# Seven block products for z, operand sums made earlier, and a turned fold loop in an attention and two-MLP kernel on one core

## The chip, the cores and the metric

One core of a Trainium2 chip runs the whole program. The metric is device time in microseconds (us) of one execution, the median over runs. The engines are called PE (TensorE matmul; PEld is its weight load), DVE (VectorE), ACT (ScalarE), POOL (GpSimd) and SP (SyncE, which here issues every DMA).

## The reference

All data are float32. Retention attention with a causal decay per head, then a max-of-three MLP, then a gated MLP without activation:

```python
scores = scale * np.matmul(q, k.transpose(0, 1, 3, 2))       # batch 8, heads 8, seq 576, head_dim 64
x = np.matmul(scores * Dmat[None], v)                        # Dmat: gamma_h ** (i - j) for i >= j, else 0
# tokens: 8 * 576 = 4608, d_model 512
h = np.maximum(np.maximum(x @ w1, x @ w2), x @ w3)           # d_ff 768
z = h @ w_out
a, b = z @ v1, z @ v2                                        # second MLP, d_ff 1024
out = ((a * b) @ v3) @ v_out
```

The weights arrive as float64 bits and are turned into float32 in the kernel.

## The kernel before

Every float32 operand x of a matmul is split into hi (rounded by ACT, `copy_r` line 92) and lo = x - hi (`low` line 95, on DVE or POOL); a product is three matmuls, hi*hi, lo*hi and hi*lo. Five stages follow one another on PE.

1. **Attention and h**, in blocks of 512 tokens (9 blocks, `n_blk`). Sequences are cut in 40 chunks of up to 128 tokens. For each chunk SP loads q and k (four DMAs each, lines 265 to 273), v and k again; POOL scales q and v (lines 306 to 310), DVE turns q and k (line 314), PE makes scores, output and state (lines 321 to 346), ACT and DVE write the block's x as hi and lo. `products` (line 408) makes one of 18 groups per block (6 feature tiles f, 3 weights i) of 12 matmuls of 512 columns; `maximum` folds the three into `hb`, and `keep` (line 428) stores it to `h_d` in DRAM. Beside this, `convert` (line 144) brings the other weights from float64 to float32 in 46 units (`rest`, lines 229 to 236): load `raw`, two ACT and three DVE instructions, store: 6 units of w_out to `wo1_d`, 16 of the gated weights to `wp_d`, 8 of v_out to `wo2_d`, 16 of v3 to `w3t_d` (four loads each, a DVE transpose).
2. **z = h w_out**, in 12 blocks `j` of 384 tokens (lines 616 to 642): for each of 6 feature tiles k and 4 output tiles m one `product` of three matmuls of 384 columns. `load_h` and `split_h` (lines 477 to 500) keep a ring of h tiles; DVE and POOL take turns on `hl`. Beside it the sums of the gated weights are made (`sums_of`, lines 546 to 571) and then the operands of the fold are loaded.
3. **The fold** w4 = v3 v_out (lines 715 to 728): 8 output tiles m, each 8 products of 512 columns in one bank, one after another.
4. **a and b**, in 6 pairs of 384-token blocks, by seven block products in place of eight (lines 851 to 913), and a*b to `g_d`.
5. **out = g w4**, by seven block products of 256 columns (lines 951 to 977), 18 steps `s` of 84 matmuls.

Each engine runs its instructions in program order, SP's queue included. The order of the first two blocks is written out by hand in `ORDER` (lines 30 to 48); from the third block on `when(t, fn)` gives each step a due time, in units of one group of 12 matmuls (18 to a block), and steps are emitted in the order of due times (a "+" in `ORDER` takes the next of them). For a chunk whose scores are due at t the q and k loads stand at t - 6, POOL's scaling at t - 3, DVE's turns just behind.

## Time and profile before

| | us |
|---|---|
| median of 3 runs | 1321.61 |
| runs | 1320.63, 1321.61, 1325.02 |
| the profiled execution | 1317.18 |
| its span, first to last instruction | 1315.4 |
| PE busy in the span | 1296.0 |
| stage 1, up to about | 580 |
| stage 2 (z) | 580 to 731 |
| stage 3 (fold) | 731 to 775 |
| stages 4 and 5 | 775 to 1315 |

The stage times are from the chain of waits, by the tile that PE writes (`ps_h`, `ps_z`, `ps_w`, `ps_x`/`ps_y`/`ps_v`). The granted clock is 1.00 over the whole span. A busy PE includes modelled ends of matmuls, so the distance from one matmul to the next is better read as a stretch divided by its count. SP's issues are not in the table of busy time; they stand in the timeline of its queue.

### The profile page before, as it was taken

The page shows a single profiled execution, that of the slowest core. Times are in us where ns is not written, and L with a number is a line of the kernel's source. Part 1 is how long each engine was busy: PE and PEld are TensorE (multiplying, and loading weights), DVE is VectorE, ACT ScalarE, POOL GpSimd, SP SyncE. Part 2 cuts the span into 40 slices and gives each one's busy share as a digit, 9 for nine tenths or more (in the row PEclk, how much of TensorE's full clock was granted, in tenths as well). Part 3 has the DMA queues.
Part 4 walks back from the last instruction along what each step waited for, and adds up shares of the span by engine and source line. Part 5 has one row for each costly group of instructions (what it writes and reads, how often), then busy time and mean ns, then how long its engine had stood idle before and what let it go on. Part 6 is the DMA issues. An engine that isn't in the chain of part 4 may idle for free.

```text
span 1315.4 us, 24550 instructions
## 1 busy us (share of the span) xinstructions
PE 1296.0 (99%) x9464; PEld 1184.1 (90%) x9464; DVE 753.4 (57%) x1134; ACT 447.6 (34%) x878; POOL 402.2 (31%) x356
## 2 busy tenths in 40 slices
PE   7999999999999999999999999999999999999998
PEld 5878888888888888889999899999999999899998
DVE  5996556766757675227644334334333436788885
ACT  3551111322222122124434333233333324455553
POOL 2112101121111210026634334333433434644433
PEclk9999999999999999999999999999999999999999
DMA  9966567878788785237557432222232232644552
GB/s 223 232 161 131 135 148 186 222 181 210 184 183 190 167 183 134 92 104 230 180 186 235 145 123 85 73 79 73 88 99 79 73 95 72 178 155 152 168 158 93
DMA packets 347748, 193.53 MB, mean 147 GB/s; under 512 B 243056, under 2 KB 321392, under 8 KB 347632
## 3 DMA queue, kind: packets, MB, share of 16 engines
q1 hardware_dynamic: 347632, 191.97, 53.8%
q8 instruction: 74, 1.21, 0.4%
q14 instruction: 42, 0.34, 0.1%
HBM read 125.85 MB, written 66.06 MB: 146 GB/s over the span
## 4 chain that ended last, share of the span: by engine, by line
PE 93%; DMA 2%; DVE 2%; issue 1%; SPq 1%; POOL 0%; ACT 0%; DVEq 0%; POOLq 0%; ACTq 0%
PE ps_h L416 33%; PE ps_x L584 23%; PE ps_y L584 11%; PE ps_z L584 9%; PE ps_v L584 5%; PE ps_w L584 3%; PE sc L321 2%; PE o L334 2%; PE st L346 1%; PE o L340 1%; SPq L99 1%; DMA z_d<-zo 0%; DMA w<-w_d 0%; DMA raw<-in_moe_w_dram 0%; DMA a<-wp_d 0%
## 5 line engine op out<-in xcount | busy, mean ns | idle before, releaser
L416 PE MATMUL ps_h<-xh,w1h 128*128 128x512 f32 (+1 forms) x664 | 258.5, 391 | 0.0
L416 PE MATMUL ps_h<-xh,w1l 128*128 128x512 f32 (+1 forms) x664 | 254.6, 385 | 1.7 <-DVE w1l L96 1.7
L416 PE MATMUL ps_h<-xl,w1h 128*128 128x512 f32 (+1 forms) x664 | 174.1, 384 | 0.0
L416 PEld LDWEIGHTS ps_h<-xh,w1h 128*128 128x128 f32 x664 | 124.7, 188 | 29.3 <-issue 3.6
L416 PEld LDWEIGHTS ps_h<-xh,w1l 128*128 128x128 f32 x664 | 124.8, 188 | 26.1 <-DVE w1l L96 2.4
L310 POOL TENSOR_TENSOR v<-v,tables 128x512 f32<-128x512 f32 x40 | 44.7, 1117 | 329.6 <-DMA v<-in_v_dram 310.2
L416 PEld LDWEIGHTS ps_h<-xl,w1h 128*128 128x128 f32 x664 | 123.0, 188 | 24.8
L426 DVE TENSOR_TENSOR hb<-ps_h,hb 128x512 f32<-128x512 f32 (+1 forms) x110 | 74.3, 676 | 114.0 <-PE ps_h L416 113.6
L880 POOL TENSOR_TENSOR c<-c 128x384 f32<-128x384 f32 x72 | 81.9, 1138 | 174.5 <-DVE c L748 81.7
L743 ACT ACTIVATE snap<-ps_x 128x384 f32<-128x384 f32 x120 | 58.4, 491 | 190.8 <-PE ps_x L584 185.9
L584 PE MATMUL ps_z<-hh,w1oh 128*128 128x384 f32 x288 | 96.3, 334 | 0.8 <-issue 0.8
L584 PE MATMUL ps_z<-hl,w1oh 128*128 128x384 f32 x288 | 96.3, 334 | 0.3 <-DVE hl L96 0.3
L584 PE MATMUL ps_z<-hh,w1ol 128*128 128x384 f32 x288 | 96.2, 334 | 0.0
L158 ACT ACTIVATE e<-raw 128x512 f32<-128x512 f32 x64 | 42.9, 670 | 146.6 <-DMA raw<-in_moe_w_dram 96.1
L93 ACT ACTIVATE hb<-ps_h 128x512 f32<-128x512 f32 (+1 forms) x56 | 32.4, 581 | 170.1 <-PE ps_h L416 170.1
L96 POOL TENSOR_TENSOR hl<-hr,hh 128x384 fp32r<-128x384 f32 x36 | 39.3, 1093 | 78.4 <-ACT hh L93 70.6
L748 DVE TENSOR_TENSOR c<-ps_v,snap 128x384 f32<-128x384 f32 x48 | 26.6, 556 | 62.0 <-PE ps_v L584 39.9
L307 POOL TENSOR_TENSOR q<-q,tables 128x512 f32<-128x512 f32 (+1 forms) x31 | 32.7, 1054 | 91.3 <-DMA q<-in_q_dram 71.2
L328 DVE TENSOR_TENSOR p<-sc,tables 128x512 f32<-128x512 f32 (+1 forms) x80 | 47.1, 625 | 20.5 <-PE sc L321 20.3
L93 ACT ACTIVATE hh<-hr 128x384 fp32r<-128x384 f32 x72 | 36.1, 521 | 56.2 <-PE ps_z L584 24.5
L584 PEld LDWEIGHTS ps_z<-hh,w1oh 128*128 128x128 f32 x288 | 54.1, 188 | 1.2 <-issue 1.2
L584 PEld LDWEIGHTS ps_z<-hl,w1oh 128*128 128x128 f32 x288 | 54.1, 188 | 0.7 <-DVE hl L96 0.6
(215 smaller groups left out, 3353.6 us busy)
## 6 DMA issues: line engine op xcount, KB each, us to landing
g_d<-c SPq DMA_DIRECT2D x96, 192.0 KB, 1.9
raw<-in_moe_w_dram SPq DMA_DIRECT2D x34, 512.0 KB, 6.0
h_d<-hb SPq DMA_DIRECT2D x54, 256.0 KB, 3.0
gr<-g_d SPq DMA_DIRECT2D x12, 1024.0 KB, 6.0
z_d<-zo SPq DMA_DIRECT2D x12, 768.0 KB, 3.6
zr<-z_d SPq DMA_DIRECT2D x48, 192.0 KB, 3.2
out_dram<-ob SPq DMA_DIRECT2D x36, 256.0 KB, 2.1
...
```

The costliest lines, as they stand in the source:

```text
L93: nc.scalar.activation(dst, src, AF.Copy)
L96: eng.tensor_tensor(dst, full, hi.bitcast(F32), ALU.subtract)
L158: nc.scalar.activation(z["e"], raw[:, :, 1].bitcast(F32), AF.Copy, scale=2.0 ** -112)
L307: nc.gpsimd.tensor_tensor(z["q"][:, :r], z["q"][:, :r], qs[:, j, :r].unsqueeze(3).to_broadcast([P, r, G, 32]), ALU.mult)
L310: nc.gpsimd.tensor_tensor(z["v"], z["v"], vd.unsqueeze(2).to_broadcast([P, H, D]), ALU.mult)
L328: nc.vector.tensor_tensor(z[g][:c, :, :c], z["sc"][g][:c, :, :c], mask[:c, :c].unsqueeze(1).to_broadcast([c, G, c]), ALU.mult)
L416: nc.tensor.matmul(ps[:, cols], l, r, start=n == 0, stop=n == len(mms) - 1)
L426: nc.vector.tensor_tensor(hb, ps[:, cols], hb, ALU.max)
L584: nc.tensor.matmul(ps, l, r, start=start and j == 0, stop=stop and j == len(mms) - 1, skip_group_check=again)
L743: nc.scalar.activation(t, ps[:, :N2], AF.Copy)
L748: nc.vector.tensor_tensor(r, ps[:, :N2], t, ALU.add)
L880: nc.gpsimd.tensor_tensor(x, x, y, ALU.mult)
```

## The change

z is made in 9 blocks of 512 tokens, each as a 2 by 2 block product with 7 products in place of 8 (`Z_ORDER`): output features in two halves of 256, tokens in two halves of 256, the 768 features of h in two halves of 384. One product is 2 output tiles by 3 feature tiles by three matmuls of 256 columns: 18 matmuls, in two PSUM banks out of three pairs (X, V, Y). It needs h in seven forms of [128, 3, 256] per block (4 quadrants, of which one is replaced, and differences) and w_out in seven forms. Partial results are copied out by ACT (`snap_z`) and added by DVE (`keep_z`), and stored in eight pieces of 128 KB per block.

The differences of h are made on POOL beside the attention: for blocks 2 to 8 four subtractions of 256 columns per pair of feature tiles (`differences`), one of which is in place in `hb` ahead of its `keep`, and a store of 384 KB; for blocks 0 and 1 later, by two loads, four subtractions and three stores per pair (`late_differences`, six times, due in blocks 6 and 7). The feature tiles are taken in the order 0, 3, 1, 4, 2, 5 (`F_ORDER`), and the two keeps of a pair are issued together. The sums of the gated weights move from DVE in the z stage to POOL beside the conversion (`gated_unit`), and 28 finished tiles go to `ws_d` instead of 16 to `wp_d`; in the z stage they are only loaded and split (`ws_split`, 28 steps in blocks 1 to 6). The v3 units stand ahead of the v_out units, with a store of whole 2 KB runs. `raw` has 4 buffers instead of 6 and its load stands one unit earlier. All of `hl` is on DVE. The fold runs with k outside and all 8 banks open. `ORDER` is another list of the same steps. z is read back by half as many, longer loads.

```diff
 ORDER = """
-tables fv0 fq0 fk0 fv1 fq1 sv0 fk1 fv2 tq0 fq2 ga0 eq0 fk2 tk0 up0 fq3 sv1 ek0 fk3 sc0 ft0 ft1 tq1 da0 tk1 fq4 db0
...
+tables fq0 fk0 fq1 fv0 fk1 tq0 fq2 eq0 tk0 fv1 ek0 fk2 sc0 fq3 tq1 da0 sv0 db0 fq4 ou0 eq1 fv2 ft0 ga0 xh0 tk1 up0
...
-    wp_d = dram.tile([P, 2, 2, KD, 512], F32, name="wp_d")
-    h_d = [dram.tile([P, KF1, N1], F32, name=f"h_d{t}") for t in range(NT // N1)]
-    z_d = [dram.tile([P, KD, N2], F32, name=f"z_d{t}") for t in range(NT // N2)]
+    NAMES = ("a11", "a12", "a22", "s1", "s2", "s3", "s4")
+    ws_d = dram.tile([P, 2, 2, len(NAMES), 2, 256], F32, name="ws_d")
+    h_d = [dram.tile([P, KF1 // 2, 7, N1 // 2], F32, name=f"h_d{t}") for t in range(NT // N1)]
+    z_d = [dram.tile([P, KD, 2 * N2], F32, name=f"z_d{t}") for t in range(NT // N2 // 2)]
...
+    F_ORDER = [f for c in range(KF1 // 2) for f in (c, c + KF1 // 2)]
...
-            z["raw"] = cv.tile([P, 1024], I32, tag="raw", name="raw", bufs=6)
+            z["raw"] = cv.tile([P, 1024], I32, tag="raw", name="raw", bufs=4)
-            w = cv.tile([P, 512], I32, tag="w", name="w")
+            w = cv.tile([P, 512], I32, tag="w", name="w", bufs=7)
-            when(t - 3, fetch)
+            when(t - 4, fetch)
...
+    def gated_unit(t, i, c, n):
+        quads = quadrants.setdefault((i, c), {})
+        e, kk = n % 2, n // 2
+        src = words_of(f"moe2_w{i + 1}")[(2 * kk + c) * P:(2 * kk + c + 1) * P, 1024 * e:1024 * e + 1024]
+        def keep(x, w):
+            load(ws_d[:, i, :, NAMES.index(x), c], w.rearrange("p (q f) -> p q f", q=2))
+        def add(dst, x, y, op, to):
+            nc.gpsimd.tensor_tensor(quads[to], quads[x], quads[y], op)
+            quads[dst] = quads[to]
+            keep(dst, quads[dst])
+        def done(t, w):
+            x = f"a{e + 1}{kk + 1}"
+            quads[x] = w
+            if x != "a21":
+                keep(x, w)
+        convert(t, lambda raw: [(raw, src)], done)
+        if n == 3:
+            for m, sums in enumerate((("s1", "a21", "a22", ALU.add, "a22"), ("s3", "a11", "a21", ALU.subtract, "a21"),
+                                      ("s2", "s1", "a11", ALU.subtract, "a11"), ("s4", "a12", "s2", ALU.subtract, "a12"))):
+                when(t + 5.5 + 0.8 * m, add, *sums)
...
-            load(w3t_d[:, 4 * half:4 * half + 4, j, :], wt.rearrange("p (m i) -> p m i", i=P))
+        when(t + 3.2, lambda: load(w3t_d[:, j, 4 * half:4 * half + 4], z["t"].rearrange("p (m i) -> p m i", i=P)))
-    rest += [lambda t, half=half, i=i, c=c: rows_unit(
-        t, words_of(f"moe2_w{i + 1}")[c * P:(c + 1) * P, 1024 * half:1024 * half + 1024], wp_d[:, half, i, c])
-        for i in range(2) for c in (0, 2, 1, 3) for half in range(2)]
+    rest += [lambda t, i=i, c=c, n=n: gated_unit(t, i, c, n) for i in range(2) for c in range(2) for n in range(4)]
+    rest += [lambda t, j=j, half=half: w3_unit(t, j, half) for j in range(KF2) for half in range(2)]
     rest += [lambda t, k=k: rows_unit(t, words_of("moe2_w_out")[k * P:(k + 1) * P], wo2_d[:, k]) for k in range(KF2)]
-    rest += [lambda t, j=j, half=half: w3_unit(t, j, half) for j in range(KF2) for half in range(2)]
...
     def keep(t, f):
-        load(h_d[t][:, f], hbs.pop((t, f)))
+        e, c = divmod(f, KF1 // 2)
+        load(h_d[t][:, c, 2 * e:2 * e + 2], hbs.pop((t, f)).rearrange("p (n t) -> p n t", n=2))
+    def subtract(lo, hi, t2, t3, t4):
+        for to, x, y in ((t3, hi[:, 1], lo[:, 1]), (lo[:, 1], lo[:, 1], lo[:, 0]), (t2, hi[:, 1], lo[:, 1]), (t4, hi[:, 0], t2)):
+            nc.gpsimd.tensor_tensor(to, x, y, ALU.subtract)
+    diffs = {}
+    def differences(t, c):
+        d = hb_p.tile([P, 3, N1 // 2], F32, tag="d", name="d", bufs=1)
+        subtract(*(hbs[t, f].rearrange("p (n t) -> p n t", n=2) for f in (c, c + KF1 // 2)), *(d[:, n] for n in range(3)))
+        diffs[t, c] = d
+    def keep_differences(t, c):
+        load(h_d[t][:, c, 4:], diffs.pop((t, c)))
+    def late_differences(t, c):
+        x = []
+        def fetch():
+            for e in range(3):
+                x.append(cv.tile([P, 2, N1 // 2], F32, tag="w", name="w", bufs=7))
+                if e < 2:
+                    load(x[e], h_d[t][:, c, 2 * e:2 * e + 2])
+        def work():
+            lo, hi, d = x
+            subtract(lo, hi, d[:, 0], d[:, 1], hi[:, 0])
+        def store():
+            lo, hi, d = x
+            load(h_d[t][:, c, 1], lo[:, 1])
+            load(h_d[t][:, c, 4:6], d)
+            load(h_d[t][:, c, 6], hi[:, 0])
+        return fetch, work, store
...
+            elif n % 2:
+                when(k + 1.5, differences, t, n // 2)
                 when(k + 2, keep, t, f)
+                when(k + 2, keep, t, n // 2)
+                when(k + 2.2, keep_differences, t, n // 2)
+    for n in range(EARLY * KF1 // 2):
+        for dt, step in zip((-1, 3.3, 4.3), late_differences(*divmod(n, KF1 // 2))):
+            when(T_BLK * (n_blk - 3) + dt + 6 * n, step)
...
+    Z_ORDER = (("a11", "b11"), ("a12", "b21"), ("s2", "t2"), ("s1", "t1"), ("s3", "t3"), ("s4", "b22"), ("a22", "t4"))
...
+    def z_weights(c):
+        w = {}
+        def fetch():
+            for kk in range(2):
+                r = raw_h()
+                load(r[:, :2], wo1_d[:, c + kk * KF1 // 2].rearrange("p (e n) -> p e n", e=2))
+                for e in range(2):
+                    w[f"a{e + 1}{kk + 1}"] = r[:, e]
+            w["t"] = raw_h()
+        def add(dst, x, y, op, to):
+            nc.vector.tensor_tensor(to, w[x], w[y], op)
+            w[dst] = to
+        def split(x):
+            h, l = (v[:, c] for v in zp["w"][x])
+            copy_r(h, w[x])
+            low(nc.vector, l, w[x], h)
+        return [fetch,
+                lambda: (split("a11"), add("s1", "a21", "a22", ALU.add, w["t"][:, 0])),
+                lambda: (split("a12"), add("s2", "s1", "a11", ALU.subtract, w["t"][:, 1])),
+                lambda: (split("s1"), add("s3", "a11", "a21", ALU.subtract, w["t"][:, 2])),
+                lambda: (split("s2"), add("s4", "a12", "s2", ALU.subtract, w["a12"])),
+                lambda: (split("s3"), split("a22")),
+                lambda: split("s4")]
...
+            t, x = seq[n]
+            raw = hq[n] = raw_h()
+            load(raw, h_d[t][:, :, HN.index(x)])
...
+            hh, hl = hq["op", n] = [zp["p"].tile([P, KF1 // 2, half], F32R, tag=f"h{v}", name=f"h{v}", bufs=Z_RING) for v in "hl"]
             copy_r(hh, raw)
-            low(nc.vector if n % 2 else nc.gpsimd, hl, raw, hh)
-            hq[n] = hh, hl
+            low(nc.vector, hl, raw, hh)
             load_h()
...
+    for c in range(KF1 // 2):
+        for n, step in enumerate(z_weights(c)):
+            when(t_last + 0.5 + 3.4 * c + (1.2 + 0.35 * n if n else 0), step)
+    for n in range(4):
+        when(t_last + 10.8 + 0.5 * n, load_h)
+    for n in range(Z_RING):
+        when(t_last + 14.6 + n, split_h)
...
+        todo = [(i, q, x) for q in range(2) for i in range(2) for x in NAMES]
+                load(raw, ws_d[:, i, q, NAMES.index(x)])
+        def ws_split():
+            raw, (h, l) = waiting_ws.pop(0)
+            copy_r(h, raw)
+            low(nc.gpsimd if len(todo) % 2 else nc.vector, l, raw, h)
+            ws_load()
+        for _ in range(4):
+            ws_load()
+        steps = [ws_split] * (len(todo) + len(waiting_ws))
...
+        def prepare_34(*gets):
+            for split in pending:
+                split()
+            pending[:] = [get(n) for get, n in gets]
+        first_34 = [((get_w3t, 0), (get_wo2, 0)), ((get_w3t, 1),), ((get_w3t, 2), (get_wo2, 1)), ()]
...
+        def snap_z(ps):
+            t = zp["p"].tile([P, half], F32, tag="zs", name="zs", bufs=6)
+            nc.scalar.activation(t, ps[:, :half], AF.Copy)
+            return t
+        def keep_z(t, m, n, ps, other=None):
+            o = zp["p"].tile([P, half], F32, tag="zo", name="zo", bufs=5)
+            if other is None:
+                nc.scalar.activation(o, ps[:, :half], AF.Copy)
+            else:
+                nc.vector.tensor_tensor(o, ps[:, :half], other, ALU.add)
+            pair, off = divmod((2 * t + n) * half, 2 * N2)
+            load(z_d[pair][:, m, off:off + half], o)
+        for j, t in enumerate(Z_BLOCKS):
+            for n, (x, y) in enumerate(Z_ORDER):
+                bank_of = "XVXYXYX"[n]
+                fresh = bank_of not in Z
+                if fresh:
+                    Z[bank_of] = [bank8(f"ps_{bank_of}{i}") for i in range(2)]
+                ps = Z[bank_of]
+                ah, al = zp["w"][x]
+                bh, bl = hq.pop(("op", j * len(Z_ORDER) + n))
+                for i in range(2):
+                    ms = slice(i * P, i * P + P)
+                    product(ps[i][:, :half], [(ah[:, c, ms], al[:, c, ms], bh[:, c], bl[:, c]) for c in range(KF1 // 2)], fresh, True, not fresh)
+                for i in range(2):
+                    if n in (0, 2, 3):
+                        saved[n, i] = snap_z(ps[i])
+                    elif n == 6:
+                        keep_z(t, 2 + i, 0, ps[i])
+                    else:
+                        keep_z(t, *{1: (i, 0), 4: (2 + i, 1), 5: (i, 1)}[n], ps[i], saved.pop(({1: 0, 4: 3, 5: 2}[n], i)))
                 split_h()
-                if k in slots and steps:
+                if j and n % 3 != 2 and steps:
                     steps.pop(0)()
...
-            if j == n2 - 5:
+            if j == n_blk - 3:
                 for step in steps:
                     step()
                 sx.close()
-                steps = open_34()
-        for step in steps:
-            step()
+                steps = []
+                open_34()
+            elif j == n_blk - 2:
+                steps = [lambda gets=gets: prepare_34(*gets) for gets in first_34]
...
-                        load(r[:, kk, e], z_d[2 * pair + e][:, 2 * kk + c])
+                for kk in range(2):
+                    load(r[:, kk].rearrange("p e t -> p (e t)"), z_d[pair][:, 2 * kk + c])
...
-        for m in range(KF2):
-            th, tl = w3t.pop(m)
-            ps = bank8("ps_w")
-            product(ps, [(th[:, k], tl[:, k], oh[k], ol[k]) for k in range(KF2)])
...
+        for n in range(2 * KF2):
+            k, e = divmod(n, 2)
+            th, tl = w3t.pop(n)
+            for m in range(4 * e, 4 * e + 4):
+                if k == 0:
+                    ps_w.append(bank8(f"ps_w{m}"))
+                product(ps_w[m], [(th[:, m % 4], tl[:, m % 4], *wo2[k])], k == 0, k == KF2 - 1)
+                if k == KF2 - 1:
+                    t = w4_p.tile([P, DM], F32, tag="w4", name="w4")
+                    copy_r(t, ps_w[m])
+                    load(w4_d[:, m], t)
+            prepare_34(*[(get_w3t, n + 3)] * (n + 3 < 2 * KF2), *[(get_wo2, k + 2)] * (e == 1 and k + 2 < KF2))
+            if steps:
+                steps.pop(0)()
```

## Rows read from the trace of the kernel before

**Rows 1.** The page, section 1: busy time, share of the span, instructions of each engine.
```profile
PE 1296.0 (99%) x9464; PEld 1184.1 (90%) x9464; DVE 753.4 (57%) x1134; ACT 447.6 (34%) x878; POOL 402.2 (31%) x356
```
**Rows 2.** Windows: stretch, then per engine busy (count), PEclk, DMA share, GB/s; opening and attention.
```profile
0.00:50.00 50.00, 38.85 (x565) 32.96 (x566) 33.76 (x61) 20.40 (x35) 9.11 (x14) 1.00 1.06 233
...
340.00:380.00 40.00, 40.00 (x350) 32.77 (x352) 27.87 (x45) 9.46 (x17) 5.23 (x5) 1.00 0.68 165
380.00:420.00 40.00, 40.00 (x316) 32.78 (x309) 27.52 (x43) 9.88 (x17) 6.38 (x6) 1.00 0.92 195
...
460.00:500.00 40.00, 40.00 (x362) 32.91 (x357) 28.27 (x46) 9.62 (x17) 4.24 (x4) 1.00 0.88 195
```
**Rows 3.** Windows again: the whole z stage, and fifteen periods of the last stage.
```profile
580.00:731.00 151.00, 150.09 (x864) 149.79 (x865) 77.84 (x89) 65.08 (x132) 73.74 (x60) 1.00 0.60 195
1148.94:1298.35 149.41, 149.41 (x1263) 149.41 (x1262) 127.82 (x166) 78.90 (x166) 63.89 (x45) 1.00 0.50 156
```
**Rows 4.** The chain in order of time: start, duration, what; the fold.
```profile
731.26 43.56 PE ps_w L584 x192
```
**Rows 5.** Timeline of SP's queue, 440 to 449 us: start, us, DMA issues merged.
```profile
440.69 2.75 SPq L99 DMA_DIRECT2D q<-in_q_dram  x4
443.48 2.67 SPq L99 DMA_DIRECT2D k<-in_k_dram  x4
446.25 2.16 SPq L99 DMA_DIRECT2D raw<-in_moe_w_dram  x4
448.51 0.44 SPq L99 DMA_DIRECT2D w3t_d<-w3t  x1
```
**Rows 6.** Who SP's queue waited for, 176 to 503 us: total us, times, longest.
```profile
SPq L99 <- DVE w L168: 11.8, 6, 4.7
SPq L99 <- DVE m L163: 9.7, 7, 5.2
SPq L99 <- ACT e L158: 8.3, 5, 2.4
SPq L99 <- ACT xh L93: 3.0, 1, 3.0
```
**Rows 7.** Timelines of SP and PE: two groups of k loads, the scores they feed.
```profile
340.18 2.97 SPq L99 DMA_DIRECT2D k<-in_k_dram  x4
...
487.73 2.67 SPq L99 DMA_DIRECT2D k<-in_k_dram  x4
...
365.95 1.05 PE L321 MATMUL sc<-qt,kt 64*64 64x128 f32 x32
...
503.20 1.05 PE L321 MATMUL sc<-qt,kt 64*64 64x128 f32 x32
```
**Rows 8.** DMA issues by tile: engine op xcount, KB each, median us to landing.
```profile
k<-in_k_dram SPq DMA_DIRECT2D x100, 64.0 KB, 2.6
```
**Rows 9.** Groups by line and shape: xcount | busy us, mean ns | idle before, releaser.
```profile
L314 DVE STREAM_TRANSPOSE kt<-k 128x512 f32<-128x512 f32 x25 | 26.7, 1068 | 0.0
...
L96 DVE TENSOR_TENSOR hl<-hr,hh 128x384 fp32r<-128x384 f32 x36 | 32.3, 897 | 36.0 <-ACT hh L93 36.0
...
L96 DVE TENSOR_TENSOR w1ol<-wr,w1oh 128x512 fp32r<-128x512 f32 x3 | 2.0, 682 | 0.0
...
L935 DVE TENSOR_TENSOR ob<-ps_y,snap 128x256 f32<-128x256 f32 x18 | 7.4, 411 | 5.3 <-PE ps_y L584 5.3
...
L93 ACT ACTIVATE w1oh<-wr 128x512 fp32r<-128x512 f32 x6 | 3.4, 624 | 0.0
...
L931 ACT ACTIVATE snap<-ps_x 128x256 f32<-128x256 f32 x36 | 13.5, 374 | 18.8 <-PE ps_x L584 18.8
...
L307 POOL TENSOR_TENSOR q<-q,tables 128x256 f32<-128x256 f32 x6 | 4.2, 703 | 20.1 <-DMA q<-in_q_dram 16.3 <-DVE m L164 3.9
```
**Rows 10.** Windows of five us inside the z stage and at its start.
```profile
595.00:600.00 5.00, 5.00 (x31) 5.00 (x30) 4.51 (x5) 1.57 (x3) 2.89 (x2) 1.00 0.96 309
620.00:625.00 5.00, 5.00 (x30) 5.00 (x30) 3.93 (x5) 2.38 (x5) 3.57 (x3) 1.00 1.00 359
```

More of the change, by code (lines that the diff above doesn't have):

```diff
@@ L96, in low, with load @@
         eng.tensor_tensor(dst, full, hi.bitcast(F32), ALU.subtract)
-    def load(dst, src):
-        nc.sync.dma_start(out=dst, in_=src)
+    def load(dst, src, eng=None):
+        (eng or nc.sync).dma_start(out=dst, in_=src)
     first_ps = ctx.enter_context(ExitStack())
@@ L453, in tile_retention_maxout_bilinear @@
     n2 = NT // N2
-    def open_z():
-        right.close()
-        cv_x.close()
-        p = zp["p"] = bx.enter_context(tc.tile_pool(name="zp", bufs=1, side="right"))
-        zp["w"] = [(p.tile([P, DM], F32R, name=f"w1oh{k}"), p.tile([P, DM], F32R, name=f"w1ol{k}")) for k in range(KF1)]
+    half = N1 // 2
+    HN = ("b11", "t1", "b21", "b22", "t2", "t3", "t4")
+    AN = ("a11", "a12", "a22", "s1", "s2", "s3", "s4")
+    Z_ORDER = (("a11", "b11"), ("a12", "b21"), ("s2", "t2"), ("s1", "t1"), ("s3", "t3"), ("s4", "b22"), ("a22", "t4"))
     def splitter(pool, src, hi, lo, eng, tag, bufs):
@@ L469, in splitter, with open_z, raw_h @@
         return split
-    def get_w1o(k):
-        return splitter(zp["p"], wo1_d[:, k], *zp["w"][k], nc.vector if k % 2 else nc.gpsimd, "wr", 2)
-    H_RING, H_AHEAD = 4, 4
+    def open_z():
+        right.close()
+        cv_x.close()
+        p = zp["p"] = bx.enter_context(tc.tile_pool(name="zp", bufs=1, side="right"))
+        zp["w"] = {x: [p.tile([P, KF1 // 2, half], F32R, name=f"z{x}{v}") for v in "hl"] for x in AN}
+    def raw_h():
+        return zp["p"].tile([P, KF1 // 2, half], F32, tag="hr", name="hr", bufs=4)
@@ L475, in tile_retention_maxout_bilinear @@
+    Z_RING = 3
     hq = dict(loaded=0, split=0)
+    Z_BLOCKS = list(range(n_blk))
+    seq = [(t, x) for t in Z_BLOCKS for _, x in Z_ORDER]
     def load_h():
         n = hq["loaded"]
-        if n < n2 * KF1:
+        if n < len(seq):
             hq["loaded"] = n + 1
-            j, k = divmod(n, KF1)
-            raw = hq[n] = zp["p"].tile([P, N2], F32, tag="hr", name="hr", bufs=H_AHEAD)
-            t0, done = j * N2, 0
-            while done < N2:
-                blk, off = divmod(t0 + done, N1)
-                m = min(N1 - off, N2 - done)
-                load(raw[:, done:done + m], h_d[blk][:, k, off:off + m])
-                done += m
+            t, x = seq[n]
+            raw = hq[n] = raw_h()
+            load(raw, h_d[t][:, :, HN.index(x)])
@@ L503, in tile_retention_maxout_bilinear @@
     when(t_last, open_z)
-    for k in range(KF1):
-        z = {}
-        when(t_last + 1 + 1.5 * k, lambda z=z, k=k: z.update(split=get_w1o(k)))
-        when(t_last + 4 + 1.5 * k, lambda z=z: z["split"]())
-    for n in range(H_AHEAD):
-        when(t_last + 11 + 0.5 * n, load_h)
-    for n in range(2):
-        when(t_last + 15 + n, split_h)
+    for c in range(KF1 // 2):
[5 more added lines that the diff above has]
+        when(t_last + 14.6 + n, split_h)
     with tc.manual_schedule():
@@ L586, in tile_retention_maxout_bilinear @@
         t34x = ctx.enter_context(ExitStack())
[L587 to L599 removed]
+        t34, w3t, wo2 = {}, {}, {}
@@ L707, in tile_retention_maxout_bilinear @@
         steps = [halves[0][0], waiting] + halves[0][1:] + [halves[1][0], waiting] + halves[1][1:]
[L708 to L728 removed]
+        w4x = ctx.enter_context(ExitStack())
+        w4_p = w4x.enter_context(tc.tile_pool(name="w4", bufs=6, side="right"))
+        ps_w = []
+        for n in range(2 * KF2):
+            k, e = divmod(n, 2)
+            th, tl = w3t.pop(n)
[10 more added lines that the diff above has]
+                steps.pop(0)()
         for step in steps:
             step()
+        w4x.close()
         t34x.close()
```

148 lines of the change are left out of this document (42 added, 106 removed).

## The prediction

> **What bounds the kernel now.** I read the busy times first: PE works for 1296.0 of the span of 1315.4 us [rows 1], so a change pays only where it takes matmul time away, and costs only where it makes PE wait. The windows then say where PE waits at all: 11.15 of its 19.4 idle us lie in the first 50, and in the attention stretches shown it is busy for all of the 40 us [rows 2]. The z stage is as dense: 864 matmuls in 150.09 busy us of 151 [rows 3]. The granted clock is 1.00 in each of these windows, that is 2.4 GHz. So the gain is a count of matmuls, and all else is the question whether the new side work makes a dense PE wait. Three readings answer that: SP's queue in the attention stage [rows 5 to 8], the durations of ACT, DVE and POOL [rows 9], and what the DMA moved when it was full [rows 10].
>
> **The z stage's matmuls.** Before: 12 blocks x 6 x 4 x 3 = 864 of 384 columns, 150.1 us, 173.7 ns each [rows 3]. After: 9 blocks x 7 products x 2 tiles x 3 x 3 = 1134 of 256 columns. The last stage is made of matmuls of 256 columns with the same three-term products, two banks taken up again later, and its pitch is 149.41 / 1263 = 118.3 ns [rows 3]. That gives 1134 x 118.3 = 134.2 us, **15.9 us less**. PE's weight load is busy for the whole of that stretch too (149.41 of 149.41 us) [rows 3], so at 256 columns a load is no longer shorter than its matmul; the pitch already holds that. The Trainium skill ("TensorE: Matmul & The Clock Gate", section "LDWEIGHTS (loading the stationary operand)") speaks against narrower products: a load costs columns / 1.2 ns, an estimated 107 ns for 128, as much as 256 columns stream at 2.4 GHz. If loads were not hidden, an estimated 1134 x 214 ns = 243 us would stand in place of 150; the row of 118.3 ns says that they are hidden.
>
> **The z stage's side work.** A block now takes 126 x 0.1183 = 14.9 us. ACT copies 7 operands of 768 columns, 8 partial results of 256 and 5 weight tiles of 512; 256 columns take 0.374 us and 512 take 0.624, so 768 take about 0.87: 7 x 0.87 + 8 x 0.374 + 5 x 0.624 = 12.2 us [rows 9]. DVE: 0.411 and 0.682 us give 0.95 for 768; 7 x 0.95 + 6 x 0.411 + 2.5 x 0.682 = 10.8 us [rows 9]. `hl` of 384 columns took 0.897 us beside a working POOL where the two rows give 0.55 alone [rows 9]; POOL now has 2.5 lows a block in place of half of `hl`, some 3 us, so DVE grows by at most 2 us. Both fit in 14.9. A split is issued three products ahead: after product n come the snaps (up to 0.75 us), the copy (0.87) and the low (0.95), 2.6 us, and product n+3 starts 4.26 us after n's end. I take nothing; if the chain ran longer than 4.26 us, each block would stretch (a rival).
>
> DMA: a block loads 7 x 384 KB of h, stores 8 x 128 KB of z and, in blocks 1 to 5, loads 5 x 256 KB of weight sums: 5.1 MB in 14.9 us, 343 GB/s. Before, the full windows show 309 GB/s at a share of 0.96 and 359 at 1.00 [rows 10], so such a block needs 14.2 to 15.9 us: nothing, or 1.0 us more in five or six blocks. Four h loads are in flight ahead, 8.5 us of PE, which takes up most of it. I take **1 us**, ends 0 and 6.
>
> **The attention stage.** PE's own work there is the same, only f's order differs. Added are DMA issues on SP: ahead of the last scores 18 of the stores of differences (0.39 MB), some 24 of the 30 late transfers (1.05 MB per five) and 12 more stores of sums (0.26 MB): 54 issues, 15.2 MB. Moved are v3's units, all of which now stand ahead of the last scores, where before about three stood behind them. SP's queue matters since it has hardly a gap: from 440.69 to 448.95 four rows follow each other within 0.1 us [rows 5]. And it was losing ground: the k loads of one chunk were issued by 343.15 us and its scores ran at 365.95, a lead of 22.8; ten chunks later 490.40 and 503.20, 12.8 [rows 7]. A chunk needs a landing of 2.6 us [rows 8] and a turn of 1.07 [rows 9]; 9.1 us are left.
>
> Cost at the low end, where SP's issue is what counts: 54 x (0.44 + 0.1) [rows 5] = 29.2 us, and three v3 units more, each 2.16 - 0.57 us (one issue instead of four, at a quarter of 2.16) = 1.6, 4.8 in all: 34 us. At the high end, where the data count: 15.2 MB at 309 to 359 GB/s [rows 10], 45.5 in the middle, plus 4.8: 50 us. Against that stand SP's waits in the same stretch, 11.8 + 9.7 + 8.3 + 3.0 = 32.8 us [rows 6], which a later queue doesn't have to wait again, and the 9.1: 41.9 us. So PE waits 0 to 8 us. The DMA share there is 0.68 to 0.92 [rows 2], not full, which is nearer to the low end: I take **3 us**. The Trainium skill ("DMA: Bandwidth & Descriptors", section "Issuing engines are not separate DMA queues") says that the time to issue is usually small beside the DMA itself. By it only the data would count; here four issues of 64 KB take 2.67 us [rows 5], and the row decides.
>
> The subtractions: 7 x 3 x 4 on POOL beside the attention and 6 x 4 late, 108 of 0.703 us [rows 9] = 76 us, and 16 additions of 512 columns at most twice that, 22 us: 98 us on a POOL busy for 4 to 7 of 40 us [rows 2]. They wait for DVE's last maximum of a pair; queued behind them on POOL are the scalings of q and v, on DVE the turns that wait for q, on SP the keeps and the fetches behind those. Four subtractions are 2.8 us; q's scaling has its place 3 units (about 10 us) ahead of the scores. I take nothing; DVE, at 28 of 40 us [rows 2], has room to be held up.
>
> **The rest.** The fold has the same 192 matmuls of 512 columns in 43.56 us [rows 4]; its operands are split two steps (5.4 us) ahead and ACT's copies of the finished banks (0.62 us) [rows 9] keep up with three matmuls (0.68). I take nothing, up to 2 if a bank or an operand is late. The z reads become fewer: off the path. Opening: the first q is now fetched ahead of the first v, 0.25 MB, 1.1 us at 233 GB/s [rows 2], but more v and k stand ahead of the first h products in the new list. I take 0, ends -1 and +4, since 11.15 us of waiting there [rows 2] show that the list matters.
>
> **Sum.** 1315.4 - 15.9 + 3 + 1 = 1303.5 of span; the execution is 1.8 longer than its span, 1305.3; the profiled run of before (1317.18) lay 4.4 below the median of 1321.61, so **1309.7 us**.
>
> **Rivals.**
> (B) *The attention queue falls behind.* If only a third of SP's waits can be won back, 50 - 11 - 9 = 30, with two thirds 50 - 22 - 9 = 19: PE would wait 13 to 27 us in place of 3, **1320 to 1334 us**, slower at its middle. It decides where the lead from the k loads to the scores falls under the 3.7 us of landing and turn. For it: a lead that shrank by 10 us over ten chunks [rows 7] with less in the queue, and PE idle nowhere to hide it. Against it: 32.8 us of waits [rows 6], and the windows' share under 0.92 [rows 2].
> (C) *The z stage waits for DMA.* 6 us in place of 1: **1314.7**, up to 1320 if it also meets late stores. For it the 309 GB/s window [rows 10], against it the four loads ahead.
> (D) *The operands of z come late*, since one DVE now makes every `hl` behind ACT's copy: at 1.6 to 2 us more a block, 9 blocks: **1324 to 1328**. For it: ACT at 12.2 of 14.9 us; against it the 4.26 us of lead. That the products don't come cheaper is this case too, as PE would then run at the operands' rate.
> (E) *The new opening list* costs 4 to 8 us: **1314 to 1318**.
>
> **How the numbers follow.** Forecast (PE waits 0 to 8 us in the attention, 0 to 2 in z: 1305 to 1316) 0.52; B 0.23; C 0.08; D 0.11; E 0.06. The measurement can tell about 0.3% from no change, 1317.6 to 1325.6. Faster: 0.52, of C 0.06, of E 0.04: 0.62. Same: of B 0.10, D 0.04, C 0.02, E 0.02: 0.18. Slower: of B 0.13, of D 0.07: 0.20. The range leaves out the upper half of B and the end of D above it and little below: 1304 to 1326; the forecast's own range is 1305 to 1316.
>
> **What would show it.** z's stretch in the chain: 134 us for 1134 matmuls, 118 ns each; more means C (DMA share at 1.00 in its windows, the splits waiting for `hr`) or D (PE waiting for DVE `hl` with `hr` landed). Between 130 and 580 us PE without gaps; if B holds, PE waits for DVE `kt` or POOL `v`, SP's queue has no waits left and the last lead is under 4 us. The fold at 43.6 us. The opening's idle PE at 10 to 15 us. I am wrong if the z stretch falls by less than 12 us, or if PE's waits before 580 us grow by more than 8.

## The result, and the profile after

The changed kernel takes **1333.88 us** (median of 4 runs, 1333.05 to 1337.02) against 1322.15 of the kernel before beside it: ratio 1.009, interval 1.0066 to 1.0115, so 0.9% slower. The profiled execution took 1334.54 us, its span is 1332.8. The profiled execution of the kernel before (1317.18 us) was 5 us quicker than that kernel's median and quicker than all its other executions on record (1319.26 to 1326.34). So the spans compared here differ by 17.4 us where the medians differ by 11.7, and the record doesn't show in which stage a usual execution of the kernel before spends those 5 us.

Stage ends are read on PE's timeline: its columns are start, duration, instruction, and in brackets the idle time ahead with what ended it. Here is where the first product of z follows the last of the attention:

```profile
602.22 0.39 PE L445 MATMUL ps_h<-xl,w1h 128*128 128x512 f32 x1
603.54 0.36 PE L670 MATMUL ps_X<-hh,za11h 128*128 128x256 f32 x1 [0.94 <-issue]
```

The last stretches of the attention and of z in the chain of the kernel before (start, duration, what), then those of z and of the fold in the changed kernel:

```profile
519.70 60.08 PE ps_h L416 x264
608.61 122.65 PE ps_z L584 x706
```
```profile
742.60 2.17 PE ps_X L670 x18
756.68 32.72 PE ps_w L670 x142
```

So the attention stage ends at 602.6 us, before at 579.8: **+22.8**. z ends at 744.8 in place of 731.3. It takes 141.2 us from its first matmul; with the gap ahead of it that is 9.4 less than before; the fold ends at 789.4 (774.8), +1.1; stages 4 and 5 add 2.4 and the end 0.5. Sum: 22.8 - 9.4 + 1.1 + 2.4 + 0.5 = 17.4, the difference of the spans.

Windows of the attention (columns as in [rows 2]), the same three stretches as there:

```profile
340.00:380.00 40.00, 40.00 (x370) 32.52 (x369) 27.98 (x46) 8.80 (x16) 17.26 (x16) 0.95 0.92 214
380.00:420.00 40.00, 40.00 (x348) 32.68 (x347) 26.52 (x41) 9.23 (x16) 12.93 (x13) 1.00 0.89 214
...
460.00:500.00 40.00, 34.50 (x305) 28.04 (x304) 23.99 (x38) 9.22 (x17) 19.38 (x24) 0.96 0.93 236
```

PE, full before, loses 5.5 of the last 40 us; between 130 us and the end of the stage it waits 16.4 us, before not at all. The DMA share was 0.68, 0.92 and 0.88, now 0.92, 0.89 and 0.93. The granted clock falls too, behind three of PE's stops (4.97 us at 337.67, 2.11 at 432, 2.52 at 476):

```profile
337.00:344.00 7.00, 6.33 (x28) 4.69 (x28) 5.37 (x10) 1.75 (x3) 6.01 (x6) 0.51 0.98 180
432.00:437.00 5.00, 4.57 (x80) 3.95 (x80) 4.47 (x8) 2.35 (x4) 2.10 (x3) 0.66 0.70 121
477.00:481.00 4.00, 4.00 (x55) 3.42 (x53) 2.04 (x3) 0.86 (x2) 1.75 (x2) 0.57 1.07 309
```

A mean of 0.51 says that it stood at 1.2 GHz in place of 2.4 for nearly all of that window. By PE's busy time in them the three windows cost some 6.4 us. So 16.4 us of waiting and 6.4 of clock, less the 2.3 that PE idles less ahead of 130 us (9.2 after 11.5), give 20.5 of the 22.8; the rest is not accounted for.

What SP's queue waited for between 176 and 503 us (total, times, longest), the stretch of [rows 6]:

```profile
SPq L99 <- POOL w L226: 8.1, 3, 7.4
SPq L99 <- DVE w L170: 5.5, 2, 2.9
SPq L99 <- ACT hb L93: 1.9, 1, 1.9
...
SPq L99 <- ACT e L160: 1.2, 1, 1.2
SPq L99 <- DVE m L165: 1.0, 3, 0.4
```

The waits for the converted weights (DVE w and m, ACT e) shrank from 29.8 us to 7.7, all of SP's waits in that stretch from 40 us to 28: the queue runs late. The stop at 337 us shows how that reaches PE, on the timelines of SP, POOL, DVE and PE:

```profile
326.03 2.90 SPq L99 DMA_DIRECT2D q<-in_q_dram  x4
...
332.20 1.05 POOL L336 TENSOR_TENSOR q<-q,tables 128x512 f32<-128x512 f32 x1 [6.99 <-DMA q<-in_q_dram]
...
333.29 1.09 DVE L343 STREAM_TRANSPOSE qt<-q 128x512 f32<-128x512 f32 x1 [9.09 <-POOL q L336]
...
336.95 0.67 DVE L455 TENSOR_TENSOR hb<-ps_h,hb 128x512 f32<-128x512 f32 x1
...
337.67 0.79 PE L445 MATMUL ps_h<-xh,w1h 128*128 128x512 f32 x1 [4.97 <-DVE hb L455]
```

q is issued at 326; POOL waits 7 us for it, DVE's turn waits 9 us for POOL, the maximum that frees a PSUM bank stands behind the turn on DVE, and PE runs out of banks. The scores are not what waits.

### The profile page after: what moved, and what is told of

The parts are those of the page before. It is cut to its first block, busy times and chain, and to the rows that moved or that the text cites. A ratio compares the mean times of both kernels' runs of the same rounds, so it can differ in the third digit from the quotient of the medians.

```text
span 1332.8 us, 25488 instructions
## 1 busy us (share of the span) xinstructions
PE 1295.0 (97%) x9734; PEld 1178.6 (88%) x9734; DVE 788.9 (59%) x1217; ACT 479.4 (36%) x932; POOL 454.0 (34%) x429
## 3 DMA queue, kind: packets, MB, share of 16 engines
q8 instruction: 76, 1.25, 0.4%
## 4 chain that ended last, share of the span: by engine, by line
PE 53%; DMA 8%; SPq 5%; DVE 2%; issue 2%; ACT 1%; POOL 1%; DVEq 0%; ACTq 0%; POOLq 0%
PE ps_x L670 23%; PE ps_y L670 11%; PE ps_h L445 6%; PE ps_v L670 6%; SPq L99 5%; DMA z_d<-zo 4%; PE ps_w L670 2%; PE ps_X L670 2%; PE ps_Y L670 1%; DMA q<-in_q_dram 1%; DMA w<-h_d 1%; ACT hh L93 1%; DMA raw<-w3t_d 1%; DMA w3t_d<-w3t 1%; DMA w<-w_d 0%
## 5 line engine op out<-in xcount | busy, mean ns | idle before, releaser
L96 DVE TENSOR_TENSOR hl<-hr,hh 128x768 fp32r<-128x768 f32 x63 | 62.8, 1000 | 50.3 <-ACT hh L93 44.4
L463 POOL TENSOR_TENSOR d<-hb 128x256 f32<-128x256 f32 x42 | 34.4, 818 | 151.6 <-DVE hb L455 111.9
L343 DVE STREAM_TRANSPOSE qt<-q 128x512 f32<-128x512 f32 (+1 forms) x31 | 30.0, 968 | 65.3 <-POOL q L336 58.4
L93 ACT ACTIVATE hh<-hr 128x768 fp32r<-128x768 f32 x63 | 53.2, 845 | 18.8 <-DMA hr<-h_d 6.1
L166 DVE CUSTOM_DVE_ANT_0 m<-m,r 128x1024 uint16<-128x1024 uint16 x64 | 51.1, 799 | 6.7 <-ACT r L161 0.2
L844 DVE TENSOR_TENSOR c<-ps_x,snap 128x384 f32<-128x384 f32 x48 | 25.4, 552 | 49.0 <-PE ps_x L670 49.0
L93 ACT ACTIVATE xh<-o 128x512 fp32r<-128x512 f32 (+1 forms) x40 | 22.1, 552 | 80.7 <-PE o L369 56.8
```

Source lines behind the costliest of these rows:

```text
L93: nc.scalar.activation(dst, src, AF.Copy)
L96: eng.tensor_tensor(dst, full, hi.bitcast(F32), ALU.subtract)
L166: nc.vector.tensor_tensor(z["m"], z["m"], z["r"], ALU.add)
L844: nc.vector.tensor_tensor(r, ps[:, :N2], t, ALU.add)
```

## The experiments

Theories: the attention stage loses its time to **issues** (SP's time per instruction), to **bytes** (the DMA engines), to **POOL** (subtractions ahead of the scalings), or to **order** (q and k too late in the queue). In z it is **DMA or the ring** of z tiles against **operands**. Three kernels with the same attention code (the changed one, z2, z3) ended it at 602.6, 602.7 and 605.0, so 2.4 us there is scatter. In z, the kernels with the changed kernel's z code and as many bytes (the changed one, x1 to x4, y1, y2) took 140.4 to 145.6 us. Each run that is named has one trace.

**Leaving parts out of the changed kernel.**

x1_no_late:
```diff
-    for n in range(EARLY * KF1 // 2):
-        for dt, step in zip((-1, 3.3, 4.3), late_differences(*divmod(n, KF1 // 2))):
-            when(T_BLK * (n_blk - 3) + dt + 6 * n, step)
...
-            load(raw, h_d[t][:, :, HN.index(x)])
+            load(raw, h_d[max(t, EARLY)][:, :, HN.index(x)])
```


> The six late units (12 loads, 24 POOL subtractions, 18 stores of the differences of blocks 0 and 1) are left out; the z stage reads blocks 2 and 3 in their place, so the number of its loads is the same. In the changed kernel PE's last product of the attention stage ends at 602.6 us, in the kernel before at 579.8. Theory queue (what is issued on SP or moved by DMA in blocks 6 and 7 makes q, k and v late): the PE gaps behind 420 us (some 11 us of waiting and 3 us of lowered clock) go, those at 337 us stay: the stage ends at 586 to 592 and the span falls by 11 to 16 us. Theory POOL order (the subtractions of blocks 2 to 8 alone hold up the scalings of q and v): little changes, 597 to 603.

The stage ends at 592.7 us: -9.9. The stop at 337 stays (3.4 us), those behind 420 shrink. Time 1322.1 us.

x2_thin:
```diff
-        load(h_d[t][:, c, 4:], diffs.pop((t, c)))
+        load(h_d[t][:, c, 4:, :32], diffs.pop((t, c))[:, :, :32])
...
```


> The 21 stores of differences and the 18 late stores are issued as before in number and rows, but each row carries 128 bytes in place of 1 KB: about 10 MB less moved, the same issues on SP. The z stage reads the whole quadrants in place of the differences, as many bytes. Theory data (bytes make the q and k loads late): the attention stage ends at 583 to 592 us in place of 602.6. Theory issue (SP's time for each of the added instructions makes them late, whatever they carry): 599 to 604. Theory POOL: 599 to 604 too.

595.8 us: -6.8 with as many issues. That is neither theory's number; bytes count.

x3_no_subtract:
```diff
-            nc.gpsimd.tensor_tensor(quads[to], quads[x], quads[y], op)
...
-        load(h_d[t][:, c, 4:], diffs.pop((t, c)))
+        load(h_d[t][:, c, 4:], diffs[0])
...
-            subtract(lo, hi, d[:, 0], d[:, 1], hi[:, 0])
...
```


> All added transfers stay; the subtractions on POOL (84 beside the attention, 24 late) and the 16 sums of the gated weights are left out, a tile of zeros is stored as the differences, and the stores no longer wait for POOL. Theory POOL (scalings of q and v stand behind the subtractions, and stores on SP wait for them): the attention stage ends at 581 to 590 us in place of 602.6, and PE's waits for POOL w and d (some 6 us) go. Theory queue: the waits move to POOL q or DVE hb and the stage still ends at 597 to 603.

596.8 us: -5.8, and PE still waits 12.0 us between 130 and 620. POOL has a part, not the main one; as the stores no longer wait for POOL either, the two are not told apart.

x4_fetch_early:
```diff
-        when(t - 6, fetch_qk)
+        when(t - 9, fetch_qk)
```


> One number is changed: the q and k loads of a chunk stand 9 units ahead of its scores in SP's queue in place of 6 (some 12 us). Theory order (the queue has enough room, but DVE's turns and POOL's scalings block because q comes late): PE's gaps in the attention go, the stage ends at 581 to 590 us in place of 602.6, and the time is 1310 to 1322 us. Theory overload (the queue carries more than it can in that stage): the waits only move to other loads (v, the weights, the keeps), the stage ends at 597 to 604 and the time stays at 1330 to 1335.

600.3 us, within the scatter; the time is 1329.0 us, ratio 1.0052 (1.0035 to 1.0069). Order alone doesn't cure it.

y1_early_diffs:
```diff
+                    early(f"df{t}.{n}", differences, t, n // 2)
+                    early(f"kp{t}.{n}", keep_pair, t, n // 2)
...
```


> The differences of blocks 0 and 1 are made right behind their maxima in the opening and stored with the keeps (6 more stores, 24 POOL subtractions there); the late units (12 loads, 18 stores) go. One more hb buffer, one w buffer less. All of the computation is kept. Queue theory: as without the late units, the attention stage ends at 592 to 597 us in place of 602.6. If the opening has no room for it, PE's idle time ahead of 130 us grows from 9.2 us and the stage ends behind 597.

592.5 us, as without the late units: the opening has room for them (PE idle ahead of 130 us: 9.8, after 9.2). Loading h back to subtract was pure cost.

y2_act_stores:
```diff
-        load(h_d[t][:, c, 4:], diffs.pop((t, c)))
+        load(h_d[t][:, c, 4:], diffs.pop((t, c)), nc.scalar)
...
```


> The stores of differences, the late stores and the 28 stores of weight sums are issued from ACT's queue in place of SP's, at due times at which their data are ready; the same bytes. In the changed kernel these 66 issues took 40 us of SP's time between 130 and 600 us. Theory issue (SP's time is what runs out): the attention stage ends at 583 to 593 us in place of 602.6. Theory data (the DMA engines run out, whoever issues): 598 to 604. A third outcome, later than 604: ACT is held up by the issues and its copies come late.

600.3 us, within the scatter, though 66 issues that took 40 us of SP's time left it (they took 28 us on ACT). SP's queue now waits for transfers that have not landed (its waits, 250 to 520 us):

```profile
SPq L99 <- DMA ws_d<-w: 12.9, 8, 2.6
SPq L99 <- DMA h_d<-d: 8.0, 7, 1.8
SPq L99 <- DMA v<-in_v_dram: 5.5, 7, 2.5
```

So SP's time was not what ran out in the changed kernel. The Trainium skill ("DMA: Bandwidth & Descriptors", section "Issuing engines are not separate DMA queues") says that all issuers end on the same DMA engines and that the issuing time saved is usually small; this trace agrees: the 40 us gained 2.3. v1 below shows that many issues still cost something by themselves.

y3_sums_before (stores quadrants, sums on DVE in the z stage as in the kernel before):
```diff
-    rest += [lambda t, i=i, c=c, n=n: gated_unit(t, i, c, n) for i in range(2) for c in range(2) for n in range(4)]
+    rest += [lambda t, half=half, i=i, c=c: rows_unit(
...
```


> The gated weights are stored as quadrants again (16 stores in place of 28, no sums on POOL) and their sums are made on DVE in the z stage, where 16 loads of 256 KB (4.2 MB) take the place of 28 (7.3 MB). Theory overload of the queue in the attention: its end at 594 to 599 us in place of 602.6, all gained behind 200 us. For the z stage, which took 141.2 us: theory DMA (its windows are at a share of 0.96 to 0.99): 136 to 138 us; theory operands (ACT and DVE make the splits late, and DVE now has 16 sums more): 141 to 145.

The attention ends at 593.2 (-9.4), but z takes 157.8 us with the DMA share at 0.77 to 0.87: operands, not DMA, and worse than either theory's range. ACT waits for the first group, which is fetched one step ahead, and PE behind it:

```profile
PE ps_X L658 <- ACT zs L686: 12.3, 4, 5.2
...
ACT a22h L93 <- DMA a<-wp_d: 7.3, 1, 7.3
```

**Each load alone, on the kernel before** (attention end 579.8).

v1_before_issues, v2_before_bytes:
```diff
+    for e in range(62):
+        when(T0 + (T1 - T0) * e / 62, extra, e % 8, 32 * (e % 32), 32)
...
```
```diff
+    for e in range(30):
+        when(T0 + (T1 - T0) * e / 30, extra, e % 8, 0, 1024)
...
```


> The kernel before, with 62 small loads (128 rows of 128 bytes, 1.0 MB in all) put at even distances into SP's queue from unit 45 to 144; nobody uses what they load. Theory issue (SP's time of some 0.4 us for each instruction makes q, k and v late): the attention stage, which ended at 579.8 us, ends at 587 to 600. Theory data or POOL: 579 to 582. Theory sum (the queue has room for any one of the three): 579 to 583.

> The kernel before, with 30 loads of 512 KB (15.7 MB in 4 KB rows) at even distances from unit 45 to 144; nobody uses what they load. Half as many instructions as the change added, all of its bytes. Theory data: the attention stage ends at 587 to 600 us in place of 579.8. Theory issue: 582 to 588 at most. Theory sum: 579 to 584.

v3_before_pool (subtractions), v4_before_all (those and 62 loads of 240 KB):
```diff
+    for t in range(EARLY, n_blk):
+        for f in (1, 3, 5):
+            when(T_BLK * t + 3 * f + 2 + 1.5, differ, t, f)
...
```


> The kernel before, with 84 subtractions of 256 columns on POOL that wait for DVE's maxima as those of the change do, 24 more of them in blocks 6 and 7 and 16 of 512 columns, all into a tile that nobody uses; no transfer is added and the stores wait for nothing new. Theory POOL (the scalings of q and v stand behind them): the attention stage ends at 584 to 592 us in place of 579.8 and PE waits for POOL v. Theory queue: 579 to 582.

> The kernel before, with 62 loads of 240 KB (15.2 MB) at even distances and the subtractions of v3_before_pool: all three things that the change added beside the attention, without its dependences between them. If these loads alone explain the 22.8 us: the attention stage ends at 597 to 606 us. If it ends below 592, the change's own order (stores that wait on SP for POOL, q and k that wait behind them) matters as much as the load.

Ends: issues 588.2 (+8.4, of which 5.4 are PE waits), bytes 609.2 (**+29.4**), POOL 583.6 (+3.8, of which 1.25 is a PE wait in that stage), all 607.0 (+27.2). Half the instructions with all the bytes cost more than three times as much as all the instructions with hardly any. v1 lies in the range of theory issue all the same, v2 beyond that of data, v3 between its two. The added loads of v2 all fill one tile; SP waited 3.4 us for the one ahead. v2's end on PE's timeline:

```profile
610.00 0.41 PE L593 MATMUL ps_z<-hh,w1oh 128*128 128x384 f32 x1 [0.83 <-issue]
```

Windows of the kernel before, of v1 and of v2 from 340 to 480 us:

```profile
340.00:410.00 70.00, 70.00 (x588) 57.27 (x590) 46.97 (x74) 15.80 (x27) 9.96 (x9) 1.00 0.78 177
410.00:480.00 70.00, 70.00 (x621) 57.33 (x613) 47.05 (x80) 15.76 (x28) 11.78 (x14) 1.00 0.85 183
```
```profile
340.00:410.00 70.00, 70.00 (x571) 57.29 (x569) 48.85 (x75) 17.62 (x30) 11.08 (x10) 1.00 0.84 199
410.00:480.00 70.00, 64.74 (x560) 51.93 (x556) 41.12 (x72) 14.93 (x27) 10.40 (x13) 0.98 0.81 173
```
```profile
340.00:410.00 70.00, 70.00 (x615) 57.20 (x614) 43.92 (x71) 16.84 (x30) 9.00 (x9) 1.00 0.91 222
410.00:480.00 70.00, 60.04 (x481) 47.88 (x479) 38.29 (x66) 13.22 (x24) 10.36 (x13) 0.93 0.88 194
```

Loaded, this stage moves some 190 to 240 GB/s at shares of 0.87 to 0.93 (v2 here, the changed kernel above). Before it stood at 0.78 and 0.85 already. Over the whole stretch from 130 to 500 us, the kernel before, the changed one, v2, and z5 (a version below that moves less in all):

```profile
130.00:500.00 370.00, 370.00 (x3136) 302.96 (x3135) 238.09 (x383) 85.67 (x148) 57.44 (x62) 1.00 0.78 182
130.00:500.00 370.00, 354.85 (x2971) 289.10 (x2970) 232.88 (x369) 81.59 (x143) 137.21 (x150) 0.98 0.84 204
130.00:500.00 370.00, 352.52 (x2949) 286.29 (x2951) 214.72 (x353) 77.46 (x137) 56.01 (x59) 0.98 0.84 203
130.00:500.00 370.00, 370.00 (x3135) 302.75 (x3134) 249.72 (x393) 87.81 (x152) 122.77 (x141) 1.00 0.85 206
```

So the share doesn't tell by itself whether PE waits: it is 0.84 with 15 to 17 us of PE lost and 0.85 with none.

**The z stage.**

z2_ring7, z3_no_z_stores:
```diff
-            o = zp["p"].tile([P, half], F32, tag="zo", name="zo", bufs=5)
+            o = zp["p"].tile([P, half], F32, tag="zo", name="zo", bufs=7)
```
```diff
-            load(z_d[pair][:, m, off:off + half], o)
...
-                    load(r[:, kk].rearrange("p e t -> p (e t)"), z_d[pair][:, 2 * kk + c])
+                    load(r[:, kk].rearrange("p e t -> p (e t)"), h_d[pair][:, c, kk:kk + 3].rearrange("p n t -> p (n t)"))
```


> The changed kernel with a ring of 7 z tiles in place of 5, nothing else. ACT waited 16.2 us in 7 pieces for a tile whose store had not landed, and PE for the snaps behind it. Theory ring: the z stage takes 137 to 139 us in place of 141.2, and ACT's wait for the stores falls under 6 us. Theory DMA full: the wait moves to the loads of h and z still takes 140 to 142 us.

> The 72 stores of z (9.4 MB) are left out, and the operands of a and b are loaded from the tiles of h instead, the same bytes. Theory DMA: without them the z stage's waits go, 134 to 137 us in place of 141.2, its windows' DMA share falls to 0.7 to 0.8. Theory operands (ACT's copy of h and the one DVE that makes every hl are late): 139 to 142 us, and PE still waits for ACT zs or DVE hl.

z takes 138.0 us with two tiles more and 137.3 without stores, after 141.2; both lie under the 140.4 to 145.6 of the kernels with five tiles and the same z code. Waits in z of the changed kernel; then windows of it and of z2:

```profile
ACT zo L704 <- DMA z_d<-zo: 16.2, 7, 3.5
...
PE ps_X L670 <- ACT zs L698: 3.1, 4, 1.4
```
```profile
620.00:660.00 40.00, 39.92 (x333) 39.72 (x332) 27.62 (x40) 28.68 (x55) 9.73 (x6) 1.00 0.97 317
660.00:700.00 40.00, 39.05 (x322) 38.45 (x321) 25.08 (x38) 23.45 (x45) 9.09 (x6) 1.00 0.99 321
```
```profile
620.00:660.00 40.00, 40.00 (x336) 40.00 (x335) 25.81 (x38) 27.97 (x54) 9.95 (x6) 1.00 0.95 308
660.00:700.00 40.00, 40.00 (x335) 39.86 (x334) 28.15 (x43) 28.10 (x54) 9.80 (x6) 1.00 1.02 345
```

The same bytes fit at a share of 1.02 with PE full. The ring was the stop: ACT, out of tiles, held the snaps and so the banks. 3.2 of the 3.9 us are the ring's; the other 0.7 is within the scatter.

**Versions that move less beside the attention.**

y4_early_sums is y1 and y3 together, with q and k at `t - 8`.


> Both together, the q and k loads two units earlier, six hb buffers and two for the differences: the seven products for z and the turned fold stay, the work beside the attention is that of the kernel before and 21 plus 6 stores of differences. All of the computation is kept. If the queue's overload is the cause and its parts add up (9.9 of the late units, 2.3 of the earlier q and k, 4 to 8 of the sums), the attention stage ends at 583 to 590 us and the time is 1308 to 1317 us, below both kernels. If the differences of blocks 2 to 8 alone overload it, 590 to 597 us and 1318 to 1326.

The attention ends at 581.2 us, 21.4 earlier, so the parts add (9.9 + 9.4 + 2.3 = 21.6 of the 22.8, though the 2.3 alone is within the scatter); z takes 154.1. 1325.55 us, ratio 1.0031 (1.0018 to 1.0044).

z1_early_sums_ahead mends z (edits against y4), z4_sums_on_pool is z1 with the sums on POOL (edit against z1):
```diff
-        steps = [groups[0][0]]
+        groups[0][0]()
+        steps = []
...
-            o = zp["p"].tile([P, half], F32, tag="zo", name="zo", bufs=5)
+            o = zp["p"].tile([P, half], F32, tag="zo", name="zo", bufs=7)
```
```diff
-                nc.vector.tensor_tensor(w[to], w[x], w[y], op)
+                nc.gpsimd.tensor_tensor(w[to], w[x], w[y], op)
```


> As the kernel with early differences and sums in the z stage, with three edits: the first group of gated weights is loaded ahead of the z loop instead of in it (there ACT waited 7.4 us for it and PE 5.7 us), the ring of z tiles has 7 buffers in place of 5, and the q and k loads stand 8 units ahead only where the scores are due behind unit 54, so that the opening keeps its order. All of the computation is kept. Theory place (the z stage's 154.1 us are 134.2 plus waits from a late first load and the ring): z at 138 to 144 us, the attention stage's end at 579 to 583, the time at 1309 to 1316 us, below both kernels. Theory side work (ACT, DVE and POOL with the sums are too slow for the operands): z at 148 to 154, 1318 to 1325 us.

> As z1_early_sums_ahead, with the 16 sums of the gated weights and all 28 of their lo parts on POOL, none on DVE. If DVE's share in the sums delays hl: z 2 to 6 us shorter than in z1_early_sums_ahead. If POOL becomes the slow one, the gated splits drag behind, ACT waits for the sums in front of its copies of h, and z is 2 to 10 us longer.

z1: attention 579.9, z 143.5, **1312.25 us, ratio 0.9937 (0.9919 to 0.9955)**. z4: z 149.7, 1319.2 us, 0.9983 (0.9969 to 0.9997); ACT waits for POOL's sums in front of its copies of h (6.6, 6.1, 5.5 and 4.3 us for s3, s4, s2, s1).

z5_spread issues a group's four loads one per step (edits against z1); z6_lead6 is z1 with q and k at `t - 6`:
```diff
-            steps += g[1:3] + ([groups[n + 1][0]] if n + 1 < 4 else []) + g[3:]
+                    if n + 1 < 4 and 1 <= m <= 4:
+                        groups[n + 1][0](*quarters[m - 1])
...
```


> As z1_early_sums_ahead, with the four loads of a group of gated weights (256 KB each) issued one per step in place of four in a row. Theory burst: ACT's 12.0 us of waiting for h (the raw tile hr) shrink, PE's gaps in z (4.6 us) fall under 2, z takes 138 to 141 us in place of 143.5 and the time is 1307 to 1311 us. Theory side work: z stays at 142 to 146 us.

> As z1_early_sums_ahead, with the q and k loads at 6 units ahead of the scores everywhere, as in the changed kernel. Theory bytes (with 7 MB fewer moved the DMA engines keep up): the attention stage ends at 579 to 582 us as with 8 units. Theory lead: PE waits for DVE hb again and the stage ends at 584 to 590.

z5: z 142.0 us (PE waits 3.7 there, not under 2), **1310.31 us, ratio 0.9915 (0.990 to 0.993)**, below both kernels. That it is quicker than z1 is not shown: the intervals overlap, and z6, with z1's z code, took 142.9 there. z6: the attention ends at 582.6, between its theories, with one PE wait of 2.08 us at 445: moving less gives most of it, the lead at most some 3 us, near the scatter. The end of the attention in z5's chain, then windows of z5:

```profile
559.93 19.04 PE ps_h L422 x84
```
```profile
340.00:420.00 80.00, 80.00 (x656) 65.61 (x655) 59.22 (x93) 18.41 (x31) 24.63 (x26) 1.00 0.89 195
420.00:500.00 80.00, 80.00 (x696) 65.25 (x695) 55.92 (x92) 20.21 (x36) 27.89 (x33) 1.00 0.88 232
```

## Why the prediction was wrong

**z's matmuls, -15.9: right in kind, 1.9 too cheap.** Dense, z2 starts a matmul every 120.0 ns (334 starts between 620 and 660; the window's 336 also count what reaches over its edges, and so do the 1263 of [rows 3], where 1260 start). That is 136.1 us for 1134 where 134.2 stood. The best z, 137.3, has 1.2 us more.

**z's DMA, 1 us (ends 0 to 6): mis-sized,** 3.9, and by another mechanism than rival C named: not the rate but five tiles for stores that land after 4.8 us. The ring's length is in the diff (`bufs=5`), and was not held against a landing. D didn't happen in the changed kernel, but in y3, y4 and z4 it did: sums between ACT and DVE made the operands late.

**The attention, 3 us (ends 0 to 8): the step that failed; 22.8.** What failed is the set-off of 34 to 50 us of added queue work against a credit of 41.9 us, with the low end taken. Rival B came about: its sum, 19 to 30 us, holds the 22.8 (the 13 to 27 us given beside that sum don't follow from it). Both signs of being wrong came: z's stretch fell by 9.4 us, under 12, and PE's waits grew by 16.4, over 8. In detail:
- *The low end.* SP's issues were taken as what counts, since a share of 0.92 was "not full". v1, issues with hardly any bytes, cost 8.4 us; v2, as many bytes as the change added with half the issues, 29.4.
- *The room for bytes.* 15.2 MB were priced at the 309 to 359 GB/s of [rows 10], rows of the z stage: 45.5 us. That rate was about right. These are packets, MB and the packets' share of the 16 DMA engines' time up to the stage's end, for the kernel before (579.8 us), the changed one (602.6) and z5 (579.0):

```profile
q1 hardware_dynamic: 270656, 97.97, 71.8%
q1 hardware_dynamic: 278807, 116.58, 78.6%
q1 hardware_dynamic: 270029, 109.49, 77.7%
```

The shares come to 416, 474 and 450 us. So the change added 57 us of packet time for 18.6 MB (325 GB/s; the 15.2 MB were counted to the last scores only), and z5's 34 us, with q and k 8 units ahead, fitted without a PE wait; z6's 36, with 6 units, cost one of 2.08 us. v2 added 60 us for 15.7 MB. Most packets here are short: up to that end 238108 of the changed kernel's 278865 carry under 512 bytes. The Trainium skill ("DMA: Bandwidth & Descriptors", "Specifications") asks for at least 512 bytes for the full rate; no run here changed the size of the short packets of q, k and v, so that they take up the room is argued, not shown.
- *The credit of 41.9 us.* SP's waits were taken as time that a late queue wins back in full. In all they fell from 40 to 28 us, and the last lead from 12.8 to 9.1: some 16 us came back. New waits stand among those left, as 8.1 us for POOL's sums. v1's 62 issues, priced as in the prediction, are 62 x 0.54 = 33 us, which the credit should have swallowed; they cost 8.4. Rival B's doubt was right.
- *The deadline.* B was to decide where the lead from k loads to scores falls under 3.7 us; it never fell under 8. The deadline is that of the first engine that blocks in order: DVE's turn of q, due 2.8 units ahead of the scores, with the maxima behind it. POOL q and DVE `hb` are the names in the rows, not `kt` or `v`.

**POOL's subtractions, nothing:** up to 3.8 us alone (v3, little more than the scatter), 5.8 under load (x3). That they delay q's scaling had been named and set at nothing.

**Fold, 0 to 2:** 1.1. **Opening, -1 to +4:** PE's idle time ahead of 60 us fell by 2.0. **The clock** had no term; the 6.4 us come from PE's own stops. Of the 2.4 us in stages 4 and 5, 1.6 are one stop between the two (3.25 us at 1143.9, before 1.67 at 1127.7), and the granted clock was 0.66 from 1140 to 1150 us, before 1.00 around its stop.

Set against the forecast span of 1303.5, the missing 29.3 us are 19.8 in the attention, 5.5 in z, 1.1 in the fold and 2.4 + 0.5 behind it. Set against the forecast time of 1309.7, 24.2 us are missing, since the quick profiled execution of before is allowed for there.
